# One order of transfers and early work changed: block 1's transposes directly behind the first weight halves on SyncE

## The chip, the core and the metric

The kernel runs on one core of one Trainium2 chip. The metric is the device time of one execution in microseconds, the median over several runs. A profiled execution gives the trace from which all rows below come.

## The reference, cut to what matters

The input `x` is 2048 rows of 512 numbers in bfloat16. It is normalised per row, and the sum of three terms is returned:

```
xn  = layernorm(x)                                # 2048 x 512
qkv = xn @ wqkv                                   # 512 x 1536; 32 heads of 16
o   = softmax over 8 keys at distances 0,2,..,14  # sliding, dilated, masked before the start
B   = (gelu(xn @ w_gate) * (xn @ w_up)) @ w_down  # 512 -> 1376 -> 512
out = x + o @ wo + B
```

## The kernel before, in words

**Tiles.** The 2048 rows are four blocks of 512 (block 0 to 3), each of two loads of 256 rows (`x0` to `x7`; the first two loads in halves) and of four tiles of 128 rows (t = 0 to 15). `xnT` holds the normalised block transposed, three buffers in turn; TensorE reads it for every product. Block 0 is transposed on TensorE (`tpx`, `tpy`, L888 and L877) and copied out of PSUM by ScalarE and VectorE (`evx`, L910; `evy`, L902). The other blocks are transposed by DMA, 128 rows at a time, on SyncE: `trx2_0`, `trx2_1`, `trx3_0`, `trx3_1` make block 1 (L860).

**Norms.** For tiles 0 to 7 VectorE computes the statistics (`bnst`, L717), aggregates them (`bnag`, L743), subtracts the mean (`sub`, L828), inverts the root (`rstd`, L770 and L806; the root `sq` is on ScalarE, L753 and L773) and multiplies (`norm`, L840). A transpose `trx` of a tile waits for its `norm`. For later tiles ScalarE takes the sums: `bnst8` to `bnst11` (L736) read `x4` and `x5`, and `bnag` with them is a square sum (L782).

**Attention of a block.** q and k for block 0 come tile by tile (`mmt0_t` for q, `mmt1_t` for k, L952 and L966; out of PSUM by `evq0_t`, `evk0_t`, L988), v in four pieces (`mmv`, L1010; `evv0`, L1020); for the other blocks in groups of four 128x512 matmuls (`mm1_which_g` with which 0 for q, 1 for k, 2 for v; L1035, copied out at L1046). VectorE multiplies q with the eight shifted k (`pr`, L1066), adds halves (`pa`, L1078), TensorE reduces over the head (`er`, L1102 and L1109, after which the logits lie in PSUM), and then follow the mask (block 0, L1132), `lc` (ScalarE, L1138), the maximum (`d1`), `exp`, the sum (`d4`), `ln`, `d5`, `d6`, a trip through DRAM (`ss`, `sl`), and on VectorE `pv`, `pw`, `pz` (L1217 to L1237), which leaves `OT`.

**The gated part of a block.** `fg` and `fu` (L1255) are gate and up products of 128 columns each, four matmuls; `gelu` and `uev` (L1265, L1272) bring them out of PSUM, `h` (L1279) multiplies. Columns 0 to 639 of the weights come with the loads `ld_wg0` and `ld_wu0`, columns 640 to 1279 with `ld_wg1` and `ld_wu1` (L657), the last 96 with `ld_wt0` to `ld_wt2` (L665): products j = 0 to 4 need the first halves, j = 5 to 9 the second, j = 10 (`fg0_10`, L1294, and a part of `er0_3`) the tails. `acc` (L1347) multiplies by `w_down` and `wo`.

**What sets the order.** Nothing is scheduled on the chip: `ORDER` lists the names of all steps for each engine, written out, and each engine executes its list in order, with a wait for what a step needs. SyncE's list (`sp`) issues all DMAs; a step that waits there holds up all behind it. A planner walks through the lists with a cost for each step only to give out buffer slots (PSUM has eight) and to find which waits are needed; `nbytes` is such a cost. `x4` takes the buffer of `x0`, `x5` that of `x1`, `x6` that of `x2`.

Of the kernel before, what the change touches and what calls it, by code (L numbers as in the profile page):

```python
# [96 lines left out]
class Graph:  # L97
# [250 lines left out]
    def report(self):  # L348
# [14 lines left out]
ORDER = {  # L363
    "pe":
        "warm0 warm1 warm2 warm3 warm4 warm5 warm6 warm7 warm8 warm9 tpx0_0 tpy0_0 warm10 warm11 warm12 "
        "warm13 warm14 mma0_0 tpx0_1 tpy0_1 mmb0_0 mma0_1 mmb0_1 mmt1_0 tpx1_0 mmt1_1 mmt0_2 tpx1_1 mmt1_2 "
        "mmt1_3 mmt0_3 mmv0_1 fg0_0 fg0_1 fu0_0 fu0_1 fg0_2 fu0_2 mmv0_0 mmv1_0 fg0_3 fg0_4 mm1_0_1_0 fg0_5 "
        "fu0_3 mm1_1_0_0 mm1_1_1_0 mm1_0_0_0 fg1_0 er0_3 fu0_4 fg1_1 mm1_1_3_0 fu1_0 mm1_1_2_0 fu0_5 fg0_10 "
        "mm1_0_3_0 mm1_0_2_0 fu1_1 mm1_2_0_0 fg0_6 fg1_2 fu0_6 mm1_2_2_0 fg0_7 fu1_2 fg1_3 fu1_3 mm1_2_1_0 "
        "fu0_7 fg1_4 fg1_5 mmv1_1 fg1_6 fg0_8 mm1_2_3_0 fu1_4 fu1_5 fu0_8 fu1_6 fg1_7 er1_3 fg1_8 fg1_9 fg0_9 "  # L370
        "fu0_9 fu1_7 mm2_0_1_0 fu1_8 fu1_9 mm2_0_0_0 mm2_1_3_0 mm2_1_0_0 mm2_0_3_0 mm2_1_2_0 mm2_0_2_0 "
        "mm2_1_1_0 fg2_0 fu2_0 accd1 fg2_1 fu2_1 fg2_2 accd2 fg1_10 fg2_3 mm2_2_2_0 fu2_2 fg2_4 fg2_5 acca0 "
# [4 lines left out]
        "fu3_9 acca8 accb8 accd9 accd10 acca12 accd15_1 accb12 accd15_0 accd14_0 accd11 accd13 accw15_0 "  # L377
        "accw13 accw15_1 accw14_0 accw12 accd14_1 accw14_1 accd15_2 accw15_2",
    "act":
        "c_tbl sx1 sq0 negm1 sxx1 evx0_0 sq1 evx0_1 evq0_0 sq2 evq0_1 evx1_0 sq3 evk0_1 evk0_0 evx1_1 bnst8 "  # L380
        "evk0_2 bnst9 sq4 sq6 ve8 evq0_3 evq0_2 evk0_3 vp8 gelu0_0 bnag8 halo1 bnag9 uev0_1 bnst10 va8 "
        "gelu0_2 evv0_0_0 evv0_0_1 vb8 bnst11 uev0_2 uev0_0 gelu0_1 ve10 gelu0_4 vp10 evv0_1_0 bnag10 gelu0_3 "
        "evq1_1_0 uev0_3 evk1_0_0 bnag11 gelu0_5 bnst12 va10 evk1_1_0 lc0 evq1_0_0 uev0_4 uev0_10b uev0_10c "
        "evk1_3_0 exp0 uev0_5 evk1_2_0 uev0_10a evq1_3_0 uev1_0 ln0 d5_0 evq1_2_0 gelu0_10 vb10 gelu1_2 "
        "gelu1_1 sub8 evv1_2_0 sub11 uev0_6 uev1_1 norm8 gelu1_0 uev1_3 gelu0_7 uev1_2 sub10 sub9 uev0_7 "
        "gelu1_3 gelu0_6 gelu1_4 evv1_0_0 evv1_1_0 evv0_1_1 norm11 gelu1_6 gelu1_5 gelu0_8 norm10 uev1_5 "
        "bnst13 uev1_4 norm9 ve12 vp12 uev0_8 lc1 uev1_6 bnag12 bnag13 gelu0_9 uev0_9 gelu1_7 uev1_7 gelu1_9 "
# [8 lines left out]
        "evv3_3_0 uev3_10a uev3_6 uev2_9 uev2_8 gelu3_6 gelu3_7 uev3_9 gelu3_9 gelu3_8 gelu3_10 fe8 uev3_8 "  # L396
        "fe9 fe10 fe11 fe13 fe12",
    "dve":
        "c_wdz bnst0 bnag0 sub0 rstd0 norm0a norm0b mean1 sub1 evy0_0 rstd1 norm1a norm1b bnst2 evy0_1 bnag2 "
        "sub2 rstd2 norm2 bnst3 bnag3 sub3 rstd3 norm3 bnst4 bnag4 bnst5 bnst6 bnag5 bnst7 bnag6 bnag7 sub4 "  # L400
        "sub7 sub6 rstd6 rstd4 sub5 norm6 norm4 norm7 norm5 pr0_0 pr0_1 pa0 rstd8 h0_1 h0_0 mask d1a_0 d1b_0 "
        "d1c_0 d2_0 pr1_0 d4a_0 d4b_0 d4c_0 h0_2 d6_0 pr1_1 h0_10 pa1 h1_0 rstd10 pb1 h0_3 h1_1 pv0_0 pv0_1 "
        "d1a_1 h1_2 d1b_1 pw0_1 d1c_1 h0_4 d2_1 h1_4 pw0_2 d4a_1 pz0 d4b_1 d4c_1 h1_3 pr2_0 d6_1 pr2_1 fin1 "
        "rstd12 pa2 fin2 rstd14 pb2 h1_10 pv1_1 d1a_2 pv1_0 d1b_2 fin3 d1c_2 fin0 d2_2 h2_1 pw1_1 d4a_2 h2_10 "
# [5 lines left out]
        "c_ones c_onef c_id c_vnpad c_idb c_eps c_mhalf c_e8a c_e8b c_e8c c_e8d c_ktpad c_mask0 c_mask1 c_utz "  # L410
        "sq8 sq10 sq12 sq14",
    "sp":
        "ld_x0_0 ld_x0_1 ld_wq ld_x1_0 ld_wk ld_x3 ld_x1_1 ld_x2 ld_wv ld_x4 ld_wg0 ld_wu0 ld_x5 ld_wu1 "
        "ld_wt0 trx3_0 ld_wg1 trx2_1 trx2_0 trx3_1 ld_x6 ld_wt1 ld_wt2 ldxr1 ld_wd0 ss0_2 ss0_1 ss0_3 ss0_0 "
        "sl0_1 sl0_0 ld_x7 ld_wd1 trx4_0 sl0_3 ldxr2 ld_wo sl0_2 trx5_1 trx4_1 trx5_0 ss1_3 ss1_0 ss1_1 ss1_2 "
        "sl1_3 sl1_1 trx6_0 sl1_2 sl1_0 trx7_1 ldxr3 trx7_0 trx6_1 ldxr0 ldxr4 ss2_0 ss2_1 ss2_3 sto2 ss2_2 "
        "sl2_3 sl2_0 sto0 ldxr5 sl2_1 ldxr13 sto3 ldxr12 sl2_2 ldxr8 ldxr6 sto5 ldxr7 ldxr10 ss3_3 ss3_0 "
# [21 lines left out]
def bass_parallel_sum__sliding_local_dilated__glu_gated_geglu__prompt_kernel(nc, A_x, A_wqkv, A_wo, B_x, B_w_gate, B_w_up, B_w_down, out, dbg=None, cfg=None):  # L439
# [43 lines left out]
    with contextlib.ExitStack() as es:  # L483
        block = es.enter_context(nc.Block())

        def sb(name, shape, dt):
            return es.enter_context(nc.sbuf_tensor(name, shape, dt))
# [13 lines left out]
        mask = sb("mask", [32, 2, 4, 16], F32)  # L501
# [143 lines left out]
        for i, nm in enumerate(("q", "k", "v")):  # L645
            def mk(i=i):
                return lambda e: e.dma_start(
                    Wqkv[:, :, i * 512:(i + 1) * 512],
                    A_wqkv[:, i * 512:(i + 1) * 512].rearrange("(k p) n -> p k n", p=128))
# [4 lines left out]
        for (nm, Wx, I_w, src, h) in (("g", Wg, I_wg, B_w_gate, 0), ("u", Wu, I_wu, B_w_up, 0),  # L654
                                      ("g", Wg, I_wg, B_w_gate, 1), ("u", Wu, I_wu, B_w_up, 1)):
            def mk(Wx=Wx, src=src, c=slice(640 * h, 640 * h + 640)):
                return lambda e: e.dma_start(Wx[:, :, c], src[:, c].rearrange("(k p) n -> p k n", p=128))  # L657
            t_w = G.task("sp", "ld_w%s%d" % (nm, h), 0, mk(), wr=[(I_w, h)], prio=R_WG + (nm == "u") + 0.1 * h,
                         nbytes=(640, 720)[nm == "g" and h == 0] * 1024)
            t_w.deps.add(t_ld["wk"])  # L660
            t_ld[nm] = t_w
        for (i, src, c0, c1, o) in ((0, B_w_gate, 1280, 1376, 32), (1, B_w_up, 1280, 1312, 0),
# [26 lines left out]
        for p in range(NP):  # L689
# [119 lines left out]
            for t2 in range(2):  # L809
# [33 lines left out]
                if t < 2:  # L843
                    for h in range(2):
# [5 lines left out]
                        nm = "norm%d%s" % (t, "ab"[h])  # L850
# [14 lines left out]
            for grp in ((0,), (1,)):  # L865
                n = len(grp)
                nm = "%d_%d" % (p, grp[0])
# [68 lines left out]
        for b in range(NB):  # L936
# [257 lines left out]
            for sj in range(4):  # L1194
                def mk_ss(sj=sj, itp=it_pb, b=b):
# [4 lines left out]
                       nbytes=60 * 1024)  # L1200
# [120 lines left out]
            for ti in range(4):  # L1321
# [15 lines left out]
                for ci, (c0, c1) in enumerate(cparts):  # L1337
# [59 lines left out]
                    def mk_so(t=t, it=it_ob, c0=c0, c1=c1, CW=CW):  # L1397
                        return lambda e: e.dma_start(out2[128 * t:128 * t + 128, c0:c1], OB[:, it.slot, 0:CW])
                    G.task("sp", "sto" + sfx, 0, mk_so(), rd=[it_ob], wr=[(I_out, (t, ci))], prio=base + 62,
                           nbytes=64 * CW)  # L1400
# [61 lines left out]
```

## Time and profile before

| | |
|---|---|
| median of 4 runs | 183.6 us (183.28 to 183.66) |
| profiled execution | 183.59 us, span 181.5 us |
| TensorE, VectorE, ScalarE, GpSimd busy | 176.8, 168.8, 132.6, 17.7 us |
| DMA | 19.60 MB, mean 108 GB/s |

The span is what the trace covers; the difference to the execution's time lies before and after it. Rows give the start and the length in microseconds, the engine (PE TensorE, PEld its weight loads, DVE VectorE, ACT ScalarE, POOL GpSimd, SPq SyncE's queue of issues), the line of the kernel and what is written from what. Brackets give the idle time ahead and what ended it. A transfer's time is that from issue to landing.

### The profile page before, as it was taken

Reading aid. Unit: us, or ns where it says so; the run is one execution under the profiler, and the core shown is the slowest. Engines: PE = TensorE matmul, PEld = TensorE weight load, DVE = VectorE, ACT = ScalarE, POOL = GpSimd, SP = SyncE. Lnnn points to the kernel's source line nnn. Section 1 sums busy time; section 2 is a strip of 40 time slices with the busy share of each in tenths; the row PEclk is TensorE's granted clock in tenths of the full one; section 3 lists DMA queues with packets and bytes.
Section 4 is the critical chain, followed back from the end, with each engine's and each line's share of the span. In section 5 each row is a group of like instructions: output and inputs, shape, how many; then the busy total and the mean of one; then the engine's idle time right before and its main releaser. Section 6 shows DMA issues by size and latency. Waiting matters only on the chain.

```text
span 181.5 us, 2787 instructions
## 1 busy us (share of the span) xinstructions
PE 176.8 (97%) x1060; PEld 90.8 (50%) x1060; DVE 168.8 (93%) x157; ACT 132.6 (73%) x270; POOL 17.7 (10%) x23
## 2 busy tenths in 40 slices
PE   8899989999999999999999999999999999999994
PEld 2796635444454445444444454444444444447464
DVE  3899997599999999999999999999999999999962
ACT  5689998799999998999886798953276676620110
POOL 6000060002400008307000000000000000000000
PEclk9999999999999999999999999999999999999999
DMA  4999961801495200002843000243060227710023
GB/s 120 363 357 336 196 123 28 293 0 36 114 229 195 58 0 4 0 2 58 180 140 78 25 14 0 74 127 121 20 211 5 58 58 218 244 58 4 0 72 101
DMA packets 27276, 19.60 MB, mean 108 GB/s; under 512 B 13856, under 2 KB 25088, under 8 KB 27264
## 3 DMA queue, kind: packets, MB, share of 16 engines
q1 hardware_dynamic: 27264, 19.44, 38.5%
q8 instruction: 8, 0.13, 0.3%
q14 instruction: 4, 0.03, 0.1%
HBM read 14.71 MB, written 3.15 MB: 98 GB/s over the span
## 4 chain that ended last, share of the span: by engine, by line
PE 87%; DMA 5%; DVE 3%; SPq 3%; ACT 0%; issue 0%; DVEq 0%
PE PS L1255 34%; PE PS L1347 29%; PE PS L1035 17%; DMA Wqkv<-in_A_wqkv_dram 2%; DMA xnT<-XIN 2%; SPq L860 2%; PE PS L1294 2%; DVE st L717 1%; PE PS L1102 1%; PE PS L1109 1%; PE PS L966 1%; DVE XIN L840 1%; DVE XIN L828 1%; PE PS L952 0%; PE PS L1010 0%; SPq L698 0%
## 5 line engine op out<-in xcount | busy, mean ns | idle before, releaser
L1347 PE MATMUL PS<-Wd,HT 128*128 128x512 bf16 (+2 forms) x209 | 40.4, 346 | 0.0
L1255 PE MATMUL PS<-xnT,Wu 128*128 128x512 bf16 x160 | 39.3, 380 | 0.0
L1255 PE MATMUL PS<-xnT,Wg 128*128 128x512 bf16 x160 | 39.1, 380 | 0.0
L1035 PE MATMUL PS<-xnT,Wqkv 128*128 128x512 bf16 x144 | 34.7, 380 | 0.7 <-DMA xnT<-XIN 0.7
L1217 DVE TENSOR_TENSOR UNI<-VN,PT 128x8192 f16<-128x8192 bf16 x8 | 35.3, 4420 | 0.0
L1066 DVE TENSOR_TENSOR UNI<-QT,KT 128x8192 f16<-128x8192 bf16 x8 | 35.2, 4419 | 0.0
L1347 PEld LDWEIGHTS PS<-Wd,HT 128*128 128x128 bf16 x209 | 19.6, 98 | 19.0
L1380 ACT ACTIVATE OB<-PS 128x512 bf16<-128x512 f32 x14 | 8.3, 594 | 24.0 <-PE PS L1347 23.1
L1272 ACT ACTIVATE UU<-PS 128x512 bf16<-128x512 f32 x40 | 23.8, 611 | 2.7 <-DVE HT L1279 1.3
L1265 ACT ACTIVATE GG<-PS 128x512 bf16<-128x512 f32 x40 | 23.0, 619 | 3.1 <-PE PS L1255 2.7
L1255 PEld LDWEIGHTS PS<-xnT,Wu 128*128 128x128 bf16 x160 | 15.3, 98 | 19.4 <-issue 0.4
L1255 PEld LDWEIGHTS PS<-xnT,Wg 128*128 128x128 bf16 x160 | 15.5, 98 | 18.3 <-ACT UU L1272 0.4
L1035 PEld LDWEIGHTS PS<-xnT,Wqkv 128*128 128x128 bf16 x144 | 16.2, 113 | 16.1 <-DMA xnT<-XIN 1.2
L799 POOL TENSOR_TENSOR sq<-ve,mhalf 128x2 bf16<-128x2 f32 x4 | 14.9, 3722 | 67.5 <-ACT ve L795 67.5
L1226 DVE TENSOR_TENSOR UNI<-UNI 128x8192 f16<-128x8192 f16 x4 | 17.7, 4420 | 0.0
L1078 DVE TENSOR_TENSOR UNI<-UNI 128x8192 f16<-128x8192 f16 x4 | 17.7, 4416 | 0.0
L1347 PE MATMUL PS<-Wo,OT 128*128 128x512 bf16 (+2 forms) x76 | 16.3, 346 | 0.0
L1279 DVE TENSOR_TENSOR HT<-GG,UU 128x1024 bf16<-128x1024 bf16 x20 | 13.3, 685 | 0.0
L1347 PEld LDWEIGHTS PS<-Wo,OT 128*128 128x128 bf16 x76 | 7.1, 98 | 6.5 <-DVE OT L1237 0.2
L1232 DVE TENSOR_TENSOR UNI<-UNI 128x4096 f16<-128x4096 f16 x4 | 9.2, 2290 | 0.1
L1046 ACT ACTIVATE VN<-PS 128x512 bf16<-128x512 f32 x12 | 7.2, 617 | 2.0 <-PE PS L1035 1.9
L1046 ACT ACTIVATE KT<-PS 128x512 bf16<-128x512 f32 x12 | 7.0, 596 | 1.8 <-PE PS L1035 1.8
(99 smaller groups left out, 180.1 us busy)
## 6 DMA issues: line engine op xcount, KB each, us to landing
PT<-pt_scratch SPq DMA_DIRECT2D x16, 256.0 KB, 4.1
out_dram<-OB SPq DMA_DIRECT2D x14, 128.0 KB, 2.0
XIN<-in_A_x_dram SPq DMA_DIRECT2D x12, 128.0 KB, 3.8
Wqkv<-in_A_wqkv_dram SPq DMA_DIRECT2D x3, 512.0 KB, 5.3
XIN<-in_A_x_dram SPq DMA_DIRECT2D x6, 256.0 KB, 5.3
Wg<-in_B_w_gate_dram SPq DMA_DIRECT2D x2, 640.0 KB, 5.8
Wu<-in_B_w_up_dram SPq DMA_DIRECT2D x2, 640.0 KB, 7.7
Wd<-in_B_w_down_dram SPq DMA_DIRECT2D x1, 1280.0 KB, 6.0
```

Source lines behind the costliest of these rows:

```text
L799: "pool", "sq%d" % t, 5.0, lambda e, t=t, n=n: e.tensor_tensor(out=sq[:, t:t + n], in0=ve[:, t:t + n], in1=mhalf[:, 0:n], op=ALU.pow),
L1035: ins = e.matmul(PS[:, 512 * it.slot:512 * it.slot + 512], lhsT=wcols(which, kt, g), rhs=xnT[:, itx.slot, kt, :], start=(kt == 0), stop=(k ...
L1046: return e.activation(out=o, in_=PS[:, 512 * it.slot:512 * it.slot + 512], func=ACTF.Identity, scale=(QSC, 1.0, 1.0)[which])
L1066: return lambda e: e.tensor_tensor(out=UNI[:, it.slot:it.slot + 2, :, :], in0=bass.AP(QT, (itq.slot * 4 + 2 * h) * 512, [[NQT * 4 * 512, 1 ...
L1078: return lambda e: e.tensor_tensor(out=UNI[:, i0.slot:i0.slot + 2, :, :], in0=UNI[:, i0.slot:i0.slot + 2, :, :], in1=UNI[:, i1.slot:i1.slo ...
L1217: return lambda e: e.tensor_tensor(out=bass.AP(UNI, ito.slot * 4096, [[NUNI * 4096, 128], [2048, 4], [512, 4], [1, 512]]), in0=bass.AP(VN, ...
L1226: return lambda e: e.tensor_tensor(out=UNI[:, i0.slot:i0.slot + 2, :, :], in0=UNI[:, i0.slot:i0.slot + 2, :, :], in1=UNI[:, i1.slot:i1.slo ...
L1255: ins = e.matmul(PS[0:M, 512 * it.slot:512 * it.slot + 512], lhsT=Wx[:, kt, j * 128:j * 128 + M], rhs=xnT[:, itx.slot, kt, :], start=(kt = ...
L1265: return lambda e: e.activation(out=GG[:, ito.slot, q, :], in_=PS[:, 512 * it.slot:512 * it.slot + 512], func=ACTF.Gelu_apprx_tanh)
L1272: return lambda e: e.activation(out=UU[:, ito.slot, q, :], in_=PS[:, 512 * it.slot:512 * it.slot + 512], func=ACTF.Identity)
L1279: return lambda e: e.tensor_tensor(out=HT[:, ito.slot, j - 1:j + 1, :], in0=GG[:, ig.slot, :, :], in1=UU[:, iu.slot, :, :], op=ALU.mult)
L1347: ins = e.matmul(PS[:, 512 * it.slot:512 * it.slot + CW], lhsT=(OT[:, ito.slot, q, ti * 128:(ti + 1) * 128] if kind == "o" else HT[:, ith. ...
```

## The change

On SyncE the four transposes of block 1 are moved up, directly behind the first halves of gate and up weights. Behind them follow the second halves (up before gate), the tails, the fifth load of x between them, the sixth (`x6`), and `ld_wd0` before `ldxr1`. The early parts of the three compute lists are ordered anew: VectorE takes the statistics of tiles 6 and 7 first and works each tile off as soon as it can, with `norm6`, `norm5`, `norm7`, `norm4` in that order; TensorE takes `mmv0_0` early and `fg0_5`, `fu0_5` later; ScalarE follows with its copies. Behind `mm1_2_0_0` on TensorE and `evq1_3_0` on ScalarE the lists are as before. No step is added or taken away, and the planner's cost of one load is changed.

```diff
 "pe":
-... mmb0_1 mmt1_0 tpx1_0 mmt1_1 mmt0_2 tpx1_1 mmt1_2
-mmt1_3 mmt0_3 mmv0_1 fg0_0 fg0_1 fu0_0 fu0_1 fg0_2 fu0_2 mmv0_0 mmv1_0 fg0_3 fg0_4 mm1_0_1_0 fg0_5
-fu0_3 mm1_1_0_0 mm1_1_1_0 mm1_0_0_0 fg1_0 er0_3 fu0_4 fg1_1 mm1_1_3_0 fu1_0 mm1_1_2_0 fu0_5 fg0_10
-mm1_0_3_0 mm1_0_2_0 fu1_1 mm1_2_0_0 ...
+... mmb0_1 mmt1_1 tpx1_0 mmt1_0 mmt1_2 tpx1_1 mmt0_2
+mmv0_0 mmt1_3 mmt0_3 mmv0_1 fg0_0 fg0_1 fu0_0 fg0_2 fg0_3 fu0_1 fu0_2 mm1_1_2_0 mmv1_0 mm1_1_0_0
+mm1_1_1_0 fg0_4 fu0_3 mm1_0_1_0 fu0_4 mm1_0_0_0 er0_3 fg0_10 fg0_5 fu0_5 mm1_0_2_0 fg1_0 mm1_0_3_0
+fu1_0 mm1_1_3_0 fg1_1 fu1_1 mm1_2_0_0 ...
 "act":
-... evx0_1 evq0_0 sq2 evq0_1 evx1_0 sq3 evk0_1 evk0_0 evx1_1 bnst8
-evk0_2 bnst9 sq4 sq6 ve8 evq0_3 evq0_2 evk0_3 vp8 gelu0_0 bnag8 halo1 bnag9 uev0_1 bnst10 va8
-gelu0_2 evv0_0_0 evv0_0_1 vb8 bnst11 uev0_2 uev0_0 gelu0_1 ve10 gelu0_4 vp10 evv0_1_0 bnag10 gelu0_3
-evq1_1_0 uev0_3 evk1_0_0 bnag11 gelu0_5 bnst12 va10 evk1_1_0 lc0 evq1_0_0 uev0_4 uev0_10b uev0_10c
-evk1_3_0 exp0 uev0_5 evk1_2_0 uev0_10a evq1_3_0 uev1_0 ln0 d5_0 ...
+... evx0_1 sq2 evq0_0 evq0_1 evx1_0 sq3 evk0_1 evk0_0 evk0_2 evx1_1
+sq6 bnst8 evq0_2 bnst9 sq4 ve8 evk0_3 vp8 evq0_3 bnag8 evv0_0_0 bnag9 gelu0_1 gelu0_2 va8 vb8
+gelu0_0 gelu0_3 evv0_0_1 uev0_0 uev0_1 evk1_2_0 uev0_2 evk1_0_0 halo1 evv0_1_0 evk1_1_0 gelu0_4
+bnst10 uev0_3 bnst11 evq1_1_0 ve10 uev0_4 vp10 evq1_0_0 bnag10 uev0_10c lc0 uev0_10a gelu0_5 bnag11
+uev0_5 va10 uev0_10b bnst12 exp0 evk1_3_0 evq1_3_0 uev1_0 ln0 d5_0 ...
 "dve":
-... bnst2 evy0_1 bnag2 sub2 rstd2 norm2 bnst3 bnag3 sub3 rstd3 norm3
-bnst4 bnag4 bnst5 bnst6 bnag5 bnst7 bnag6 bnag7 sub4 sub7 sub6 rstd6 rstd4 sub5 norm6 norm4 norm7 norm5
-pr0_0 pr0_1 pa0 rstd8 h0_1 h0_0 mask d1a_0 ...
+... bnst2 bnag2 evy0_1 sub2 rstd2 norm2 bnst3 bnag3 sub3 rstd3 norm3
+bnst7 bnst6 bnag7 bnag6 bnst4 sub6 rstd6 bnst5 norm6 bnag5 bnag4 sub7 sub5 rstd4 norm5 sub4 norm7 norm4
+pr0_0 pr0_1 pa0 rstd8 h0_0 h0_1 mask d1a_0 ...
 "sp":
-... ld_wv ld_x4 ld_wg0 ld_wu0 ld_x5 ld_wu1
-ld_wt0 trx3_0 ld_wg1 trx2_1 trx2_0 trx3_1 ld_x6 ld_wt1 ld_wt2 ldxr1 ld_wd0 ss0_2 ...
+... ld_wv ld_x4 ld_wg0 ld_wu0 trx3_0 trx2_1
+trx2_0 trx3_1 ld_wu1 ld_wg1 ld_wt0 ld_x5 ld_wt1 ld_wt2 ld_x6 ld_wd0 ldxr1 ss0_2 ...
 ...
-                         nbytes=(640, 720)[nm == "g" and h == 0] * 1024)
+                         nbytes=(640, 1070)[nm == "g" and h == 0] * 1024)
```

## The prediction

> **What bounds the kernel now.** I read the page first, then the chain that ended last, then SyncE and TensorE in order of time around the one hole, then single transfers from issue to landing.
>
> ```profile
> PE 176.8 (97%) x1060; PEld 90.8 (50%) x1060; DVE 168.8 (93%) x157; ACT 132.6 (73%) x270; POOL 17.7 (10%) x23
> PEclk9999999999999999999999999999999999999999
> ```
>
> TensorE is busy for 97% at full clock in every slice, so the end moves only with a TensorE hole or a late VectorE. The chain, in order of time:
>
> ```profile
> 15.15 1.06 DVE XIN L840 x4
> 16.21 0.54 SPq L860
> 16.75 0.05 issue
> 16.80 0.57 SPq L657
> 17.38 0.05 issue
> 17.43 1.68 SPq L860
> 19.11 0.04 issue
> 19.15 1.27 SPq L860
> 20.41 0.04 issue
> 20.46 4.18 DMA xnT<-XIN
> 24.64 0.05 issue
> 24.69 1.05 PE PS L1035 x4
> ```
>
> From 24.69 on the chain is TensorE without a hole up to 179.16, and before it lies the path of block 1: norms on VectorE, SyncE issuing transposes with a 640 KB weight load (L657) among them, and 4.18 us for the last one to land. TensorE alone:
>
> ```profile
> 22.06 1.89 PE L1255 MATMUL PS<-xnT,Wg 128*128 128x512 bf16 x8
> 24.69 1.05 PE L1035 MATMUL PS<-xnT,Wqkv 128*128 128x512 bf16 x4 [0.74 <-DMA xnT<-XIN]
> ```
>
> Groups of four 512-wide matmuls follow each other at 0.865 us (eight at 15.13, the next at 16.86). Two from 22.06 would leave room at 23.79; the next began at 24.69. The hole costs 0.90 us; the 0.74 shown is less because the modelled ends of matmuls overlap the next start.
>
> The second bound is VectorE. It waits around the reduction er0_3 and is nearly gapless after d1a_0 (33.76). At the end the last weighted values come 0.17 us before TensorE wants them:
>
> ```profile
> 172.29 1.22 DVE L1237 TENSOR_TENSOR OT<-UNI 128x2048 bf16<-128x2048 f16 x1
> 173.68 2.99 PE L1347 MATMUL PS<-Wo,OT 128*128 128x256 bf16 x20
> ```
>
> So a gain on TensorE counts only if VectorE's chain comes forward too.
>
> **The change part by part.** Instructions and bytes stay the same; only orders move. (The 1070 for 720 is a planner's number and moves no bytes.)
>
> *First transpose.* Before, it went out at 15.44 behind norm6, after all eight statistics steps. Behind norm3 (its bnst4 follower starts at 11.05) VectorE now runs bnst7, bnst6, bnag7, bnag6, bnst4, sub6, rstd6, bnst5, norm6. At the row's pitches (0.58 a statistics step back to back, 0.69 where the next needs it, 0.09 an aggregate, 0.26 a subtract or multiply, 0.08 a reciprocal) that is 2.4 + 0.2 + 0.26 + 0.08 + 0.3 = 3.2, so norm6 ends at 14.3. The whole row of eighteen steps is the same work, so norm4, now last, ends near 16.2 to 16.4. ScalarE's copy evx1_1 comes behind evk0_2, 0.5 later, at 12.25, and ends before mmt1_3 at 13.35. Two swaps further ahead cost nothing: evy0_1 goes from 7.21 to 7.43 and is still 0.25 ahead of mmb0_1 near 8.0; sq2 goes ahead of evq0_0, which moves from 7.65 to 7.7 with no reader before pr0_0. If the first cover were gone, TensorE would lose what is missing, at most 0.2.
>
> *The other three.* Each transpose holds SyncE 1.20 to 1.31 (once 1.68). From 14.3: 15.6, 16.95 (norm4 is done), 18.3 for the last issue, against 20.46; one slow issue makes it 18.7. Two reasons: the chain starts 1.1 earlier, and L657 (0.57) and the wait up to 17.43 are gone. The same transfer with a quiet queue:
>
> ```profile
> xnT<-XIN SPq DMA_TRANSPOSE x1, 2.4
> ```
>
> This is the one issued at 91.63; the four of block 1 took 4.8, 5.8, 5.1 and 4.2 behind wu1, x5 and wg1. Bounds for the last landing: 18.3 + 2.4 = 20.7 and 18.7 + 4.2 = 22.9. I take 20.9: only wu0 is still ahead of the first, landed by 16.8, and nothing but transposes is ahead of the last.
>
> *The first use.* Up to 14.26 TensorE has the same groups plus mmv0_0 (0.87), which needs wv (landed 11.5) at 12.5. mmt0_3 ends at 15.13, mmv0_1 at 16.00, seven gate and up groups take 6.05: mm1_1_2 wants block 1 at 22.05, 1.7 earlier than before. Cover: 22.05 - 20.9 = 1.15; if it is gone, each us later is a us of hole. fu0_0 wants wu0 at 17.7 instead of 16.86 and gains cover. ScalarE's first gelu waits behind bnag8, evv0_0_0, bnag9 and the table load until 19.3 (17.44 before); by then TensorE has filled six of the eight PSUM buffers (mmv0_1, fg0_0 to fg0_3, fu0_0), and from there ScalarE empties one in 0.48 while TensorE fills one in 0.865: cover of two buffers.
>
> *What now stands behind the transposes.* SyncE: wu1 19.6, wg1 20.1, wt0 20.6, x5 21.1, then wt1, wt2, x6, wd0, ldxr1. Data of wu1 starts near 20.7 (x6 shows 1.0 from issue to first data). At the 360 GB/s of the saturated slices: 1.8 each for wu1 and wg1, 0.5 for wt0, 0.75 for x5, so x5 is through at 25.6 and lands at 26 with receipt; the slowest of the 16 DMA engines lags by 0.4 to 2 us (wu0: first part 14.8, last 16.8), so 26.4 to 28. I take 27.0. Wanted: wg1 by fg0_5 at 32.1 (lands near 25), wt2 by er0_3 at 30 (27 to 28.7), both covered. x6 is wanted by bnst12 at 35. ld_wd0 goes out 7 us earlier and ldxr1 later, wanted at 75.8 (first Wd group) and 85.6 (fin1): no price.
>
> The Trainium skill ("Advanced Engine Details and Errata", X-Bar Transpose) says that transposing transfers run about as fast as plain ones, 350 to 400 GB/s. By that, four of 128 KB would hold back the weights by an estimated 1.5 us, against 5.2 us of SyncE's own rows (four of 1.3); the measurement decides, and by the rule alone x5 would land an estimated 3.7 us earlier, the last transpose too, and the sum would be 182.7.
>
> *The new tight wait.* bnst10 (ScalarE, in order) reads x5. It stands behind gelu0_4, which needs fg0_4: that starts at 25.5 (22.05 plus four groups), ends at 26.55, and gelu0_4 takes 0.48: bnst10 is up at 27.0. Queued behind it: uev0_3, bnst11, evq1_1_0, uev0_4, evq1_0_0, bnag10, uev0_10c and lc0, about 4.5 us of work up to lc0 at 31.8, with some 0.3 of slack in waits for TensorE. lc0 feeds the softmax of block 0 and through it VectorE to the end. So x5 up to 27.3 costs nothing, and each us beyond costs a us less what VectorE has in hand.
>
> *er0_3 and VectorE.* Both orders put eighteen groups between 14.26 and er0_3: 14.26 + 18 x 0.866 + 0.1 of mode change = 29.95 instead of 30.85. It needs pa0: pr0_0 may start 0.0 to 0.25 late (evq0_3 is now the last copy, near 16.2), so pa0 ends at 29.4 to 29.6: covered by 0.35.
>
> ```profile
> DVE PS L1132 <- PE PS L1109: 1.8, 1, 1.8
> ACT PB L1138 <- DVE PS L1132: 1.4, 1, 1.4
> ```
>
> These waits are for er0_3, so the mask, lc0 and d1a_0 come 0.9 earlier as well. Between lc0 and exp0 stand other ScalarE steps (uev0_10a 0.6, gelu0_5 0.48, bnag11 0.71, uev0_5 0.48, va10 0.1, uev0_10b 0.4, bnst12 0.62): lc0 31.8 + 0.92 + 3.4 + table load 1.3 = 37.4, as before; it ends at 38.5, before pr1_0 (from 34.5, 4.34 long) at 38.9. Then only three copies stand before ln0 instead of five, so d6_0 comes 0.9 to 1.1 earlier: VectorE keeps up with TensorE.
>
> *Sum.* Profiled execution: 183.59 (span 181.5, 2.09 around it), equal to the median of 183.6. Hole gone -0.90; x5 at 27.0: 0; half of what a lag to 27.6 would take, +0.1: 182.8.
>
> **Rivals.**
> - *The transposes still take 4.2 us.* For it: all four did in this place, and two of the delays came with data of one slow engine that every other engine waited for. Against: what lay ahead then lies behind now. Landing 18.3 + 4.2 = 22.5 leaves a hole of 0.45: 183.15; with slow issues, 22.9 and 183.55.
> - *x5 late, ending slower.* Place: ScalarE at bnst10. For it: 1.6 MB now go ahead of x5 behind four transposes, and one DMA engine lost nearly 2 us earlier. Against: 26.4 is the plain sum. It cancels the gain from a landing at 28.4 (27.3 + 0.9 + 0.2 in hand on VectorE) on; at 29.0 the time is 184.2.
> - *The gain is taken back by VectorE* because pr0_0 or exp0 slips: with 0.17 at the end and 0.3 lost, 183.2; with all lost, 183.5, no change.
>
> **How the numbers follow.** Hole gone 0.62 (182.5 to 183.1); transposes at 4.2 us 0.10; x5 beyond 28.0, 0.14; VectorE 0.10; a wait that no row of before shows 0.04. Measurement tells about 0.2%, 0.37 us, from no change: faster means under 183.23, slower over 183.97. Faster: 0.62, 0.05 of the first and 0.03 of the third rival, 0.70. Slower: 0.12 of x5 and the 0.04, 0.16. The rest is 0.14. The range goes from 182.4 (183.28, the lowest of the four runs, less 0.90) to 183.8, which takes in the first and third rival and x5 up to its break-even and leaves out some 0.16.
>
> **What would show it.** Right: no idle before the first L1035 group, which starts near 22.05; the first L860 on SyncE near 14.3, the last near 18.3, landing 2.4 to 3 us after issue; the mask wait ends near 31.5; the reduction of block 0 at 29.95. Wrong: idle on TensorE near 22 (transposes), a ScalarE wait for the DMA of XIN near 27 (x5), or TensorE idle before the last Wo groups near 172.8 (VectorE).

## The result: 183.94 us, slower by 0.2%

The median of after is 183.94 us (38 runs, 183.14 to 184.6) against 183.49 for before, measured alongside (61 runs, 183.04 to 183.8): the ratio is 1.0021, interval 1.0014 to 1.0028. The prediction was 182.8 with a range up to 183.8; the result lies beyond it, on the side of the second rival. The profiled execution of after took 183.47 (span 181.4), at the low end of its runs and 0.12 under the profiled execution of before. So the trace read here shows how the gain was cancelled; the further half a microsecond of the median lies in executions without a trace, and whether they began later or waited longer is open.

Three of the steps named ahead of the result can be read at once. TensorE's view in order of time and SyncE's, from the profile of after:

```profile
21.66 1.03 PE L1035 MATMUL PS<-xnT,Wqkv 128*128 128x512 bf16 x4
```

```profile
13.93 5.23 SPq L860 DMA_TRANSPOSE xnT<-XIN  x4
20.93 0.70 SPq L704 DMA_DIRECT2D XIN<-in_A_x_dram  x1
```

The first group on block 1 has no bracket: the hole is gone. The four transposes were issued in 5.23 us from 13.93 on and the last landed at 20.40, 1.26 ahead of its use. (This execution ran about 0.4 ahead of the clock of the prediction, its q weights having landed by 5.67 instead of 6.20.) So the edit did what it says. ScalarE and VectorE of after show what took its place. First the rows of before, then those of after:

```profile
32.71 1.02 ACT L1138 ACTIVATE PB<-PS 128x1024 bf16<-128x1024 f32 x1 [1.37 <-DVE PS L1132]
37.45 1.06 ACT L1161 ACTIVATE EX<-PB 128x1024 f16<-128x1024 bf16 x1
```

```profile
32.39 0.29 DVE L1132 TENSOR_TENSOR PS<-PS,mask 32x128 f32<-32x128 f32 x1 [1.76 <-PE PS L1109]
33.76 0.43 DVE L1143 TENSOR_TENSOR SU<-PB 128x512 bf16<-128x512 bf16 x1 [1.09 <-ACT PB L1138]
```

```profile
26.18 0.60 ACT L1265 ACTIVATE GG<-PS 128x512 bf16<-128x512 f32 x1
28.08 0.63 ACT L736 ACTIVATE XS<-XIN 128x512 bf16<-128x512 bf16 x1 [1.30 <-DMA XIN<-in_A_x_dram]
32.67 1.02 ACT L1138 ACTIVATE PB<-PS 128x1024 bf16<-128x1024 f32 x1
38.66 1.06 ACT L1161 ACTIVATE EX<-PB 128x1024 f16<-128x1024 bf16 x1
```

```profile
31.07 0.29 DVE L1132 TENSOR_TENSOR PS<-PS,mask 32x128 f32<-32x128 f32 x1 [0.86 <-PE PS L1109]
33.73 0.42 DVE L1143 TENSOR_TENSOR SU<-PB 128x512 bf16<-128x512 bf16 x1 [2.37 <-ACT PB L1138]
```

The second row of ScalarE in after is `bnst10`, which reads `x5`. It waited 1.30 for the transfer. The mask was on VectorE at 31.07, earlier than before (32.39) by 1.3, but `lc0` (L1138) started at 32.67 (32.71 before) because ScalarE was late (no bracket: it came straight from other work), so `d1a_0` waited 2.37 for it and started at 33.73 (33.76 before). `exp0` is even 1.2 later than before (38.66 against 37.45). Nothing that was won on TensorE reached VectorE.

Two rows of TensorE in after show where the time is given back:

```profile
40.26 1.05 PE L1035 MATMUL PS<-xnT,Wqkv 128*128 128x512 bf16 x4 [0.51 <-ACT KT L1046]
44.16 1.05 PE L1035 MATMUL PS<-xnT,Wqkv 128*128 128x512 bf16 x4 [0.26 <-ACT GG L1302]
```

The chain that ended last, between 13 and 46 us, goes over to ScalarE (lines left out are marked by dots):

```profile
31.98 1.74 PE PS L1255 x8
33.72 0.58 ACT UT L1310
...
38.66 1.06 ACT EX L1161
...
43.51 0.61 ACT GG L1302
44.12 0.05 issue
44.16 1.05 PE PS L1035 x4
```

In before the chain was TensorE alone from 24.69 to 179.16; here ScalarE carries it from 33.72 to 44.12, working through what `bnst10` had held up, and TensorE waits twice for a copy out of PSUM (before 40.26 and before 44.16). So the time is lost directly between ScalarE and TensorE: those copies stand on ScalarE's list behind what was late.

### The profile page after: what moved, and what is told of

Its sections match the earlier page's. It is cut to its first block, busy times and chain, and to the rows that moved or that the text cites. A ratio compares the mean times of both kernels' runs of the same rounds, so it can differ in the third digit from the quotient of the medians.

```text
span 181.4 us, 2785 instructions
## 1 busy us (share of the span) xinstructions
PE 177.0 (98%) x1060; PEld 90.6 (50%) x1060; DVE 168.6 (93%) x157; ACT 132.8 (73%) x270; POOL 21.7 (12%) x23
## 4 chain that ended last, share of the span: by engine, by line
PE 90%; ACT 7%; DMA 1%; issue 1%; SPq 0%; DVE 0%; DVEq 0%
PE PS L1255 35%; PE PS L1347 29%; PE PS L1035 15%; PE PS L952 3%; PE PS L1294 2%; PE PS L1010 2%; PE PS L1102 1%; PE PS L1109 1%; DMA XIN<-in_A_x_dram 1%; PE PS L966 1%; ACT L1302 1%; ACT L1160 1%; ACT EX L1161 1%; ACT XR L727 1%; ACT UU L1272 1%; ACT QT L1046 1%
## 5 line engine op out<-in xcount | busy, mean ns | idle before, releaser
L1035 PE MATMUL PS<-xnT,Wqkv 128*128 128x512 bf16 x144 | 35.0, 380 | 0.8 <-ACT KT L1046 0.5
L799 POOL TENSOR_TENSOR sq<-ve,mhalf 128x2 bf16<-128x2 f32 x4 | 18.8, 4704 | 63.6 <-ACT ve L795 63.6
L1035 PEld LDWEIGHTS PS<-xnT,Wqkv 128*128 128x128 bf16 x144 | 16.1, 113 | 16.2 <-ACT KT L1046 1.0
```

The costliest lines, as they stand in the source:

```text
L799: "pool", "sq%d" % t, 5.0, lambda e, t=t, n=n: e.tensor_tensor(out=sq[:, t:t + n], in0=ve[:, t:t + n], in1=mhalf[:, 0:n], op=ALU.pow),
L1035: ins = e.matmul(PS[:, 512 * it.slot:512 * it.slot + 512], lhsT=wcols(which, kt, g), rhs=xnT[:, itx.slot, kt, :], start=(kt == 0), stop=(k ...
```

## The experiments

The theory: `x5`, now behind 1.4 MB of weights on SyncE's list, lands too late for `bnst10`, and ScalarE's delay takes back what the hole gave. The rivals: the new order of the compute lists is itself slower; VectorE is late for another reason; or the gain was never there.

**Take the wait away by moving the load up (e1).** Only `ld_x5` moves, ahead of the second weight halves (here and below, `...` marks what is left out of a list):

```diff
-"trx2_0 trx3_1 ld_wu1 ld_wg1 ld_wt0 ld_x5 ld_wt1 ld_wt2 ...
+"trx2_0 trx3_1 ld_x5 ld_wu1 ld_wg1 ld_wt0 ld_wt1 ld_wt2 ...
```

> The fifth load of x goes directly behind the four transposes, ahead of the second weight halves; nothing else differs from the changed kernel. Theory (the first statistics step on ScalarE that reads x5, bnst10, waits 1.3 us for its landing at 28.1 and gives the gain back): x5 lands near 22.5, the wait is gone, the mask-to-copy wait of VectorE falls from 2.4 to about 1.1 us, and the time is near 182.6, 0.9 under before. Rival (the gain is lost in the new ScalarE and VectorE order itself, the transposes or PSUM): time stays near 183.9. Cost by the theory: second halves land 0.75 later, still 4 us ahead of their first reader.

Measured: 182.51 us (182.37 to 182.75), ratio to before 0.9934, interval 0.9918 to 0.995. `x5` landed at 22.49. The row of `bnst10` on ScalarE and that of `d1a_0` on VectorE:

```profile
26.89 0.62 ACT L736 ACTIVATE XS<-XIN 128x512 bf16<-128x512 bf16 x1
32.73 0.43 DVE L1143 TENSOR_TENSOR SU<-PB 128x512 bf16<-128x512 bf16 x1 [1.17 <-ACT PB L1138]
```

No bracket at `bnst10`, and `d1a_0` comes 1.0 earlier than in after. The two waits of TensorE are gone too: from the group at 38.94 to the one at 44.12 it takes 5.18 us, where the same stretch of after, from 38.73 to 45.05, takes 6.32. This is the version that beats both kernels, and it differs from after by the place of one load.

**The load where it was before (e2), and in between (e7).** In e2 `ld_x5` stands behind `ld_wu0`, ahead of the transposes; in e7 between `ld_wu1` and `ld_wg1`:

```diff
-... ld_wg0 ld_wu0 trx3_0 trx2_1 trx2_0 trx3_1 ld_wu1 ld_wg1 ld_wt0 ld_x5 ...
+... ld_wg0 ld_wu0 ld_x5 trx3_0 trx2_1 trx2_0 trx3_1 ld_wu1 ld_wg1 ld_wt0 ...    (e2)
+... ld_wg0 ld_wu0 trx3_0 trx2_1 trx2_0 trx3_1 ld_wu1 ld_x5 ld_wg1 ld_wt0 ...    (e7)
```

> The fifth load of x goes back to where it stood in the kernel before, behind the first halves and ahead of the transposes. Theory: x5 lands by 17, no wait at bnst10, near 182.6. The transposes find 0.75 us more data ahead of them and land at most 0.75 later (21.1 instead of 20.4), still ahead of the first use at 21.7. Rival 1 (the order on the compute engines eats the gain): 183.9. Rival 2 (the transposes have no slack): a TensorE hole near 21.7 and 183.0 or more.

> The changed kernel with the fifth load of x between the second up half and the second gate half. Theory (x5 costs nothing while it lands before 27.0): it lands near 25 and the time is that of x5 directly behind the transposes, 182.5. Rival (every place behind the transposes delays it too much, or what counts is the number of bytes ahead): between 182.8 and 183.9.

Measured: e2 182.79 us, ratio 0.9948 (0.9931 to 0.9965), `x5` landed at 17.22, the last transpose at 21.02 against a first use at 22.28; e7 182.65 us, ratio 0.9942 (0.992 to 0.9965), `x5` at 25.11. Neither has a wait at `bnst10`. Between landings of 17.2 and 25.1 the time does not follow the landing at all: it matters only beyond some point that lies later than 25.1.

**The load later still (e3).** `ld_x5` behind the last tail:

```diff
-... ld_wt0 ld_x5 ld_wt1 ld_wt2 ld_x6 ...
+... ld_wt0 ld_wt1 ld_wt2 ld_x5 ld_x6 ...
```

> The fifth load of x goes still later, behind the two small tails of up weights. Theory: x5 lands 0.5 to 1 later than 28.1, and since ScalarE has no slack left, the time rises by as much over the changed kernel: 184.4 to 184.9. Rival (x5 is not what binds): 183.9, as the changed kernel.

Measured: 184.23 us, ratio 1.0037 (1.0023 to 1.005). `x5` landed at 28.73. Its table of waits:

```profile
ACT XS L736 <- DMA XIN<-in_A_x_dram: 1.6, 1, 1.6
DVE SU L1143 <- ACT PB L1138: 2.7, 1, 2.7
```

Both grew by 0.3 over after, and so did TensorE's first wait (0.8 for 0.5). `x5` came 0.67 later than in after, as expected, and the profiled time rose by 0.69 (184.16 for 183.47). The median, though, is only 0.29 above that of after, less than was expected, and the two intervals overlap; by the medians alone e3 and after can't be told apart.

**The same transfers, no dependence (e4).** The load stays where after has it, but `bnst10` and `bnst11` read the q weights instead of `x5`. The means of tiles 10 and 11 are then not the reference's.

```diff
-e.activation(out=XS[:, :], in_=XIN[:, it.slot, t2, :], ...
+e.activation(out=XS[:, :], in_=Wqkv[:, t2, 0:512] if t in (10, 11) else XIN[:, it.slot, t2, :], ...
```

> All orders stay those of the changed kernel, but the two sums over x5 (bnst10, bnst11) read 512 columns of the resident q weights instead, so the means of tiles 10 and 11 are not those of the reference; the next reader of x5 comes some 3 us later. Theory: the wait for the DMA at bnst10 is gone though x5 still lands near 28, and the time is near 182.6. Rival (late data on the queue, SyncE or the orders cost the time by another way): 183.9.

Measured: 182.42 us, ratio 0.9929 (0.9912 to 0.9945), with `x5` landing at 28.10 as in after. ScalarE and VectorE:

```profile
26.75 0.62 ACT L736 ACTIVATE XS<-Wqkv 128x512 bf16<-128x512 bf16 x1
31.54 1.02 ACT L1138 ACTIVATE PB<-PS 128x1024 bf16<-128x1024 f32 x1
```

```profile
32.60 0.42 DVE L1143 TENSOR_TENSOR SU<-PB 128x512 bf16<-128x512 bf16 x1 [1.18 <-ACT PB L1138]
```

The queue, the traffic and every order are those of after; only the wait is gone, and with it 1.1 us of the profiled time (182.36 for 183.47). The ratios fall further, from 1.0021 (1.0014 to 1.0028) to 0.9929 (0.9912 to 0.9945), some 1.7 us; so what the executions of after without a trace lose goes with this dependence too. The runs of after also spread over 1.46 us and those of e3 over 0.97, against 0.33 to 0.72 in the four kernels without the wait (38 and 12 runs against 6 each), which suggests, but does not show, that the length of the wait varies. That the order of the compute lists is slower by itself is out.

**The two halves of the change apart (e5, e6).** e5 keeps the new compute lists and puts the old order back around the transposes on SyncE (`ld_x5 ld_wu1 ld_wt0 trx3_0 ld_wg1 trx2_1 ...`); e6 keeps all of before's compute lists and takes the new order on SyncE, with `ld_x5` ahead of the transposes.

> The new order on the compute engines with the old order of transfers around the transposes (x5, second up half and first tail ahead of them, second gate half behind the first of them). Theory (early transposes are what the new compute order needs; x5 early costs nothing): the last transpose lands 4.2 us after its issue near 18.7, at 22.9 to 23.5, and the first use at 21.9 waits 1.0 to 1.6 us; no wait at bnst10; 183.5 to 184.1. Rival (the new compute order alone is the gain and the transposes' place does not matter): 182.6.

> The kernel before with the transfers' order alone changed: x5 in its old place, then the four transposes, then the second halves and the tails. Theory: the last transpose lands near 21.9 and the hole of 0.9 at 23.8 is gone, but the second gate half, behind four transposes, lands near 27.6 while the old TensorE order wants it at 24.7: a new hole of about 3 us, 185 to 186. Rival (the new compute order was not needed): 182.7.

Measured: e5 186.07 us (185.28 to 186.78), ratio 1.0113 (1.0072 to 1.0154); e6 186.95 us (185.48 to 188.39), ratio 1.0148 (1.0094 to 1.0203). Both medians were above what was expected, by some 2 and 1 us, and they stand for two kinds of executions: e5 took 185.28 and 185.41 at a mean granted clock of 1.000 and 186.73 and 186.78 at 0.991, e6 185.48 and 185.89 at 0.999 and 1.000 and 188.00 and 188.39 at 0.991. The traces are of the second kind. TensorE of e5:

```profile
24.67 1.90 PE L1035 MATMUL PS<-xnT,Wqkv 128*128 128x512 bf16 x4 [2.81 <-DMA xnT<-XIN]
26.36 1.71 PE L1010 MATMUL PS<-xnT,Wqkv 128*128 128x256 bf16 x8
27.90 1.89 PE L1035 MATMUL PS<-xnT,Wqkv 128*128 128x512 bf16 x8
```

The transposes landed at 24.62 (I had taken 22.9 to 23.5), and behind the hole four matmuls take 1.90 instead of 1.03. The table by slices of e5, where the last three columns are the granted clock, the DMA share and GB/s, has the granted clock beside it:

```profile
24.00:25.00 1.00, 0.33 (x1) 0.15 (x2) 0.97 (x2) 0.00 (x0) 1.00 (x1) 0.65 0.00 0
25.00:26.00 1.00, 1.00 (x4) 0.37 (x3) 1.00 (x1) 0.00 (x0) 0.23 (x1) 0.50 0.70 216
28.00:29.00 1.00, 1.00 (x7) 0.48 (x6) 1.00 (x1) 0.04 (x1) 0.00 (x0) 1.00 1.03 359
```

The clock was at half for some three microseconds. The two groups from 24.67 needed 3.23 us up to the next; the same two in after needed 1.73 (21.66 to 23.39): 1.5 us of the miss in this execution. In e6 the transposes are in time (22.43), but before's order on TensorE wants `fg0_5`, and with it the second half of the gate weights, far too early:

```profile
28.67 1.89 PE L1255 MATMUL PS<-xnT,Wg 128*128 128x512 bf16 x4 [3.97 <-DMA Wg<-in_B_w_gate_dram]
```

So neither half of the change is good alone: the new queue needs the later `fg0_5`, and the new compute order, which wants block 1 sooner, needs the new queue.

**After once more (e8).** The kernel after, unchanged:

> The changed kernel once more, unchanged, to see how its landing of x5 and its time go together. Theory: time = 182.4 + (landing of x5 - 27.0), within 0.2; a look with x5 at 28.5 gives 183.9. Rival: the spread of its times (183.1 to 184.6) has nothing to do with x5.

Measured: 183.38 us in a single run, where the expected sum gives 182.4 + 0.97 = 183.37; `x5` at 27.97, a wait of 1.21 at `bnst10`. The late landing is not one odd execution.

**Why the last part of `x5` is late (e9).** In the trace of after 15 of the load's 16 parts have landed by 27.09 and the last at 28.06. A 16 KB instruction fetch, put down to TensorE, lies at 24.35, in the middle of the load. Without the last five warming matmuls (their names leave TensorE's list too) the fetch comes about 1 us later:

```diff
-WARM = cfg.get("WARM", ([512] * 9 + [128], [128] * 5))
+WARM = cfg.get("WARM", ([512] * 9 + [128], []))
```

> The kernel after without its last five warming matmuls (which nothing reads). In the trace of after the fifth load of x has 15 of its 16 parts landed by 27.09 and the last at 28.06, and TensorE's 16 KB instruction fetch lies at 24.35, in the middle of the load. With five matmuls fewer the fetch comes about 1.1 us later by TensorE's order (5 pairs at 0.216 us). Theory that the fetch holds up one DMA engine and so one part: the last part lands elsewhere, between 27.1 and 27.6 if the fetch meets an engine whose part is already through, and the time is 182.4 + 0.1 to 0.6 = 182.5 to 183.1. Rival, the last part is late for another reason (the fetch only lies beside it): landing stays at 28.0 and the time at 183.4 to 183.9.

Measured: 185.31 us (184.77 to 186.17), ratio 1.0109 (1.0073 to 1.0146). The fetch moved to 25.55, `x5` was issued at 21.22 and landed at 28.33: 7.1 us, as in after. The landing of 27.1 to 27.6 did not come: a fetch 1.2 later still lay ahead of the last parts of `x5`, and the last of them came 0.69 behind the fifteenth (27.64). But the loads ahead of `x5` tell more. In after the fetch ran from 24.35 to 25.49, and the last part of the second gate half (`ld_wg1`) came 1.03 behind its fifteenth (27.07 for 26.04). In e9, with the fetch from 25.55 to 26.66, that load had all its parts by 26.39, the last 0.08 behind the fifteenth, and the lag began with the next load, `ld_wt0` (27.72 for 26.73). So the lag moved with the fetch, which makes the fetch the likely cause; no run is without one there. The time was a miss for both sides, for a reason that has nothing to do with it:

```profile
61.16 0.62 PE L1102 MATMUL PS<-xnT,Wt 128*32 128x256 bf16 x16 [0.97 <-ACT UU L1272]
```

The second reduction waits 0.97 for a copy out of PSUM (the trace is of an execution of 184.77), a wait that after does not have; a possible cause, which I did not try, is that five PSUM writers fewer gave the buffers out in another order.

**One sum for all of them.** TensorE's first use of block 1, taken from each trace, splits every profiled time:

| | first use | time | difference | wait of `bnst10` |
|---|---|---|---|---|
| e1 | 21.87 | 182.50 | 160.63 | none |
| e2 | 22.28 | 182.91 | 160.63 | none |
| e4 | 21.73 | 182.36 | 160.63 | none |
| e7 | 21.75 | 182.37 | 160.62 | none |
| e8 | 21.66 | 183.38 | 161.72 | 1.21 |
| after | 21.66 | 183.47 | 161.81 | 1.30 |
| e3 | 22.02 | 184.16 | 162.14 | 1.61 |

Without the wait the rest of the kernel takes 160.63, whichever place the load has. With it, 1.09 (e8), 1.18 (after) and 1.51 (e3) are lost: the wait less 0.1 each time. In e9 the difference is 162.98, that is 2.35 lost, for a wait of 1.44 less 0.1 and the 0.97 of the reduction. In e5 the first use at 24.67 and 160.63 make 185.30, which is what its executions at the full clock took (185.28 and 185.41), and the slow clock's 1.5 makes 186.8 (186.78 measured in the trace).

## Why the prediction was wrong, point by point

- *The hole: right.* The 0.90 was to go, and no L1035 group from e1 to e4 has a wait before its first use. From the four kernels without a wait, a first use at the 22.05 of the prediction gives 160.63 + 22.05 = 182.68, 0.91 under before's 183.59. By medians the gain is 0.8 (e2) to 1.2 (e4), each against before on the same chip.
- *The first use: right to 0.2.* Before's q product began at 6.33 and e2's at 6.35, but e2's first use was at 22.28, not 22.05. In e2 the first eight matmuls of q took 0.83 us where before's took 0.61, so the difference lies in that start and not in what was added up behind it.
- *The transposes: right.* 5.23 us for the issue of four, 2.5 to 3.3 us from issue to landing, against the 2.4 of the quiet queue. The last one at 20.40 is 20.79 on the prediction's clock, where 20.9 was taken. The first rival (4.2 us each) did not come. The Trainium skill ("Advanced Engine Details and Errata", X-Bar Transpose), which the prediction weighed, has transposing transfers as fast as plain ones. Here four of 128 KB took 6.5 us from the first issue to the last landing, and what stands behind them was issued at 19.20 and later: SyncE's own rows were the right price.
- *When `bnst10` is up: right.* Predicted 27.0 with a first use at 22.05, that is 4.95 behind it; after has 26.78 and 21.66, that is 5.12. Free up to 5.25 by the prediction (27.3), up to 5.2 by the table above.
- *The landing of `x5`: the step that failed.* "So 26.4 to 28. I take 27.0" is 4.95 behind the first use; measured was 28.06 at 21.66, 6.40 behind it, or 28.45 on the prediction's clock, beyond even the upper end. From issue to landing it took 7.1 instead of 5.9. Two parts of this can be read. The data started slowly: the slices of after (columns as above) have

```profile
20.00:21.00 1.00, 1.00 (x6) 0.42 (x5) 1.00 (x2) 1.00 (x3) 0.63 (x1) 1.00 0.46 35
21.00:22.00 1.00, 1.00 (x6) 0.53 (x5) 1.00 (x1) 1.00 (x3) 1.00 (x1) 1.00 0.88 221
23.00:24.00 1.00, 1.00 (x9) 0.73 (x7) 1.00 (x1) 0.81 (x2) 1.00 (x1) 1.00 1.06 391
```

  The prediction let the weights run at 360 GB/s from 1.1 behind their issue on; with `ld_wu1` issued at 19.20 that is 20.3, but in 20 to 21 only 35 GB/s went, behind the transposes, and summing the slices up to 1.67 MB brings the data through at about 26.2 instead of 25.2. And the spread: from there to the last part 1.9, where the prediction had allowed 1.4; fifteen of the sixteen parts were within that (27.09), the last was not. (The 1.6 MB that the prediction has ahead of `x5` are 1.41, and 1.67 with `x5` itself.)
- *The break-even: 0.2 too late.* The prediction gave 28.4, with 0.2 in hand on VectorE. Waits cost one for one beyond the first 0.1, so 0.91 is lost at 5.2 + 0.9 = 6.1 behind the first use, 28.2. The 0.2 in hand on VectorE was no help: TensorE lost its time in its own two waits for ScalarE's copies, not behind VectorE. And `lc0`, which frees VectorE, starts without a wait of its own even in e4 (31.54, with the mask through at 31.43), so ScalarE was the later side there already.
- *The rival had the case.* Place, mechanism and sign were those of the second rival; its 0.12 to 0.14 was too little. The break-even at 28.4 lay only 0.4 beyond the prediction's own latest landing of 28, and that range allowed for the lag of one part alone: the data ahead of it were taken as sure at 25.6, and they were 1.0 late.
- *VectorE at the end: no bound.* The third rival was not needed: in after the last weighted values start at 172.26, and TensorE wants them at 173.54 with no wait.
- *Open:* the traces account for a gain that is cancelled, 183.47 against 183.59. The median of 183.94 is 0.47 above that, and no trace shows such an execution.

## What to carry to other kernels

A load that is moved behind others is a change to whoever reads it: price its landing by the latest of its parts under the traffic that now goes ahead of it, not by bytes over peak rate, and compare that with the moment its reader is up. When two engines are balanced this closely, a gain on one counts only if every consumer between them moves too, so look for the in-order engine (here ScalarE) on which the moved datum's reader stands ahead of the critical step. A small load wanted early cost almost nothing ahead of big ones here: moving 256 KB ahead of 1.4 MB turned a loss of 0.2% into a gain of 0.7%.

## What the runs showed of the hardware

- *Half a clock after a hole of 2.8 us, in some executions.* In the traces the granted clock stayed at 1.00 over the 0.74 of idle time in before, but was 0.50 behind 2.81 in e5 and 3.97 in e6, for about three microseconds: in e5 this cost 1.5 us more than the hole itself, in e6 1.3 (the two groups from 28.67 took 3.04 up to the next at 31.71, at full clock 1.73). Two of the four executions of each had a mean clock of 0.999 or 1.000 and were 1.4 us (e5) and some 2.5 us (e6) faster. One of eleven executions of before on that chip had 0.991 as well, at 184.74 us, and has no trace. So the length of the hole alone does not decide it here. The Trainium skill ("TensorE: Matmul & The Clock Gate", HAM oscillation) warns of idle gaps above about 3.4 us. In the trace of e5, 2.81 was enough.
- *Slow data behind transposes.* Between 20 and 21 us, around the landing of the last of four transposes at 20.40, the queue of after moved 35 GB/s (44 in e8), though the second up half had been issued at 19.20; three microseconds later it moved 391. What slows the start is not shown.
- *One part of sixteen is late.* In after the last part of `x5` came 0.97 behind the fifteenth, in e9 0.69. The first load to show such a lag was `ld_wg1` in after and `ld_wt0` in e9, in both cases the first load of which no part had landed when a 16 KB instruction fetch of 1.1 us began. The fetch is the likely cause; the proof is open.
- *The start varies.* The q weights landed between 5.62 (e8) and 6.21 (e2), and the first use of block 1 in the seven rows of the table above between 21.66 and 22.28. The landing is not all of it: in e3 and e7 it was 5.90, with first uses at 22.02 and 21.75. The time follows the first use one for one, as the same table shows for the four kernels without the wait. Two profiled executions that are 0.4 apart may differ in nothing else.
